# A recurrence followed by a mixture of experts: the triangular solve taken two columns at a time, on VectorE for four of the units, with its loads issued three units ahead

## The chip, the cores and the metric

The kernel runs on one core of a Trainium2 chip. The metric is the device time of one execution in microseconds (us); lower is better. Three executions of the kernel before gave 1191.62, 1196.45 and 1198.73 us, so the median is 1196.45 us.

## What is computed

The first half is a recurrence over 768 tokens for 4 batches of 8 heads of width 40. Each token reads a 40x40 state and then updates it:

```python
for t in range(S):
    y[:, :, t] = np.einsum('bhd,bhde->bhe', rt, state)
    Sa = np.einsum('bhde,bhe->bhd', state, at)
    state_decay = state * wt[:, :, None, :] - np.einsum('bhd,bhe->bhde', Sa, bt)
    state = state_decay + np.einsum('bhd,bhe->bhde', vt, kt)
```

The second half takes the 3072 rows of y (320 wide) through four experts of hidden width 1024 and adds them up with normalized weights:

```python
for e in range(E):
    h = np.maximum(x @ w1[e], 0.0)
    out += p[:, e:e + 1] * (h @ w2[e])
```

All of it is in 32-bit floating point.

## The kernel before, in words

**Units.** The 768 tokens are cut into 12 chunks of 64. A unit is one chunk of two batches (2 x 64 tokens on the 128 partitions, 8 heads), so there are 24 units; even units hold batches 0 and 1, odd units batches 2 and 3. Inside a chunk the recurrence is turned into matrix products and one unit lower triangular system per head and batch. That system is split into 32x32 blocks: `substitute` (L433) inverts the diagonal blocks, and `merge` (L456) joins them with small matmuls.

**Stages of a unit.** `within` (L335) is a generator that prepares a unit without the state: running products of the decay (`pw`, the scan L342), scaled copies of the inputs (`gp`, `a_tok`, the reciprocal L360, `n_tok` L385, `k_tok` L388), TensorE transposes of them (`turned`: `AT`, `NT`, `KT`, `RT`, `VT`), and the score blocks (`pfe`, copied by ScalarE to `F` at L412 and masked to `ET`). `substitute` copies the diagonal blocks of `F` to `blocks` (L437), spreads them with one VectorE transpose to `M` (L441), and then runs 31 steps, one column each: a product `tmp` (L450) and an addition into `Z` (L454). Step j works on (j//4 + 1) x (31 - j) elements in each partition. Unit 0 does this on VectorE, all others on GpSimd. `merge` transposes `Z` to `Qc` and `QTc` (L461, L463) on VectorE; then come the matmuls `pY` and `pQ`. `step` (L496) applies the state: `prn`, `psat`, `pxr`, the masked copies `SX`, then `pdy`, from which the outputs `Y` and the new state are made. `Y` goes to `xT`, the input of the experts, by twelve small DMAs (L600), for unit 0 by TensorE (`pxT`, L588) instead.

**The mixture.** Units 0 and 1 go through the experts one by one (`mixture_of_unit`), the others in pairs (`mixture_of_chunk`). Its pieces stand in a list `todo`; `mix(n)` emits the next n of them between the stages of the recurrence. They fill TensorE while the recurrence waits. In each iteration of the main loop (L843) there are four places for them, `gap(0)` to `gap(3)`; in iterations 1 to 3 and at the first place of iteration 4 a gap takes one piece, later two (`sparse`, L840). Four of the gaps also hold `add_weights`, five VectorE additions of 128x640 each.

**Order.** The order of every engine follows the order in which the program emits, as a list scheduler sees it: among instructions that are ready in its own model of time, the one emitted first goes first. An instruction that isn't ready there lets a later one pass. `tc.keep_in_program_order` puts one instruction behind the one emitted before it on the same engine, and nothing more. At run time each engine keeps its order. In iteration u of the main loop the unit u takes its state step, unit u+1 is merged (`run(m, 1)` ahead of `gap(1)`), unit u+2 goes through `within` and, ahead of `gap(3)`, through `substitute`. `Qc` is pinned behind `k_tok` of unit u+2, which is the VectorE instruction emitted ahead of it.

**Loads.** Every load and store is issued from SyncE's queue (SP). A unit's inputs take 20 DMAs (L188), 2 each for W, A, B and K and 6 each for V and R. W, V and R have two buffers each, A, B and K one. The first layer's weights are loaded again for every unit or chunk, in pieces of three DMAs (L237); each piece waits for the matmuls that used its buffer.

Of the kernel before, what the change touches and what calls it, by code (L numbers as in the profile page):

```python
# [7 lines left out]
FP32 = mybir.dt.float32  # L8
# [7 lines left out]
def kernel(  # L16
# [172 lines left out]

    for u in range(3):  # L190
        begin(u)
    for u, names in ((0, "WABKV"), (1, "W"), (0, "R")):
        load(units[u], names)


# [91 lines left out]

    QUADS = ((0, 0), (1, 1), (0, 1), (1, 0))

    def turn(name, src):  # L290

        p = big(name)
        for j in range(NJ):
            nc.tensor.transpose(out=p[:, j * P:(j + 1) * P], in_=src(j), identity=ident[:])
        return p

    def tok(x):
# [37 lines left out]
    def within(q):  # L335

        n = q.n
        pw = by(turn("pw", tok(n["W"]))[:], L)
        q.G = G = sb.tile([P, 2 * NJ, L], FP32, name="G", tag="G", bufs=3)
        nc.vector.memset(G[:, :, 0:1], 0.0)  # L340
        nc.scalar.copy(out=G[:, :, 1:L], in_=pw[:, :, 0:L - 1])
        ins = nc.vector.tensor_tensor_scan(  # L342
            out=G[:].rearrange("p c i -> p (c i)"), data0=G[:].rearrange("p c i -> p (c i)"),
            data1=first[:].rearrange("p c i -> p (c i)"), initial=0.0, op0=ALU.mult, op1=ALU.add,
        )
        if q.u == 1:
            tc.keep_in_program_order(ins)
        q.gl = sb.tile([P, 2 * NJ, 1], FP32, name="gl", tag="gl", bufs=4)
        nc.scalar.copy(out=q.gl[:], in_=pw[:, :, L - 1:L])
        nc.vector.tensor_tensor(out=q.gl[:], in0=q.gl[:], in1=G[:, :, L - 1:L], op=ALU.mult)  # L350
        yield

        pg = by(turn("pg", tok(G))[:], 64)[:, :, 0:D]
        gp = sb.tile([P, H, D], FP32, name="gp")
        ins = nc.vector.tensor_tensor(out=gp[:], in0=pg, in1=n["W"][:, :, 0:D], op=ALU.mult)
        if q.u == 1:
            tc.keep_in_program_order(ins)
        A = a_tok()
        nc.vector.tensor_tensor(out=A[:, :, 0:D], in0=pg, in1=n["A"][:], op=ALU.mult)
        nc.vector.reciprocal(out=gp[:], in_=gp[:])  # L360

        def turned(name, x, keep=False):
            t = sb.tile([P, NJ, P], FP32, name=name, tag=name if keep else "turned", bufs=2 if keep else 3)
            nc.scalar.copy(out=t[:].rearrange("p j t -> p (j t)"), in_=turn("p" + name, tok(x))[:])
            return t

        def turn_rv():
            q.RT = turned("RT", n["R"], True)
            return turned("VT", n["V"])

        def causal_scores(VT):
            pc = quadrants(banks("pc"), 0, BY_TOKENS, L, lambda j, s, i: (
                d_half(j, s), i, j, of_pairs(VT, d_half(j, s), j, i), of_pairs(q.RT, d_half(j, s), j, i),
            ))
            for s in range(2):
                ins = causal(of_slot(q.VC[:], s)[:, :, D:D + L], pc[s])
                if q.start:
                    tc.keep_in_program_order(ins)

        if not q.start:  # L380
            VT = turn_rv()
            yield

        q.K, q.N = k_tok(), n_tok()
        nc.vector.scalar_tensor_tensor(  # L385
            out=q.N[:, :, 0:D], in0=n["B"][:], scalar=-1.0, in1=gp[:], op0=ALU.mult, op1=ALU.mult,
        )
        nc.vector.tensor_tensor(out=q.K[:, :, 0:D], in0=n["K"][:], in1=gp[:], op=ALU.mult)  # L388
        q.VC = VCs()
        if not q.start:  # L390
            nc.scalar.copy(out=q.VC[:, :, 0:D], in_=n["V"][:, :, 0:D])
        yield

        q.AT = turned("AT", A, True)
        NT = turned("NT", q.N)
        KT = turned("KT", q.K)
        yield

        if not q.start:
            causal_scores(VT)  # L400
            yield

        p = banks("pfe")
        pf = quadrants(p, 0, BY_TOKENS, L, lambda j, s, i: (
            s, i ^ s, j, of_pairs(q.AT, s, j, i), of_pairs(NT, s, j, i),
        ))
        pe = quadrants(p, NJ * L, BY_TOKENS, L, lambda j, s, i: (
            s, i, j, of_pairs(KT, s, j, i), of_pairs(q.AT, s, j, i),
        ))
        q.F = sb.tile([P, H, L], FP32, name="F", tag="F", bufs=2)  # L410
        for s in range(2):
            nc.scalar.copy(out=of_slot(q.F[:], s), in_=pf[s])  # L412
        ET = ETs()
        for s in range(2):
            causal(of_slot(ET[:], s), pe[s])
        yield

        if q.start:
            tc.keep_in_program_order(nc.scalar.copy(out=q.VC[:, :, 0:D], in_=n["V"][:, :, 0:D]))
        q.EV = EVs()  # L420
        pev = quadrants(banks("pev"), 0, BY_TOKENS, D, lambda j, s, i: (
            i, i ^ s, j, ET[half(i), head(j, s), :], q.VC[half(i), d_head(j, s), 0:D],
        ))
        for i in range(2):
            for p in range(2):
                nc.scalar.copy(out=of_slot(q.EV[half(p)], i ^ p)[:, :, 0:D], in_=pev[i][half(p)])
        yield

        if q.start:
            causal_scores(turn_rv())  # L430
        yield

    def substitute(q, eng):  # L433

        blocks = sb.tile([P, H, Q], FP32, name="blocks")
        for i in range(P // Q):
            ins = eng.tensor_copy(out=blocks[quarter(i)], in_=q.F[quarter(i), :, quarter(i % 2)])  # L437
            tc.keep_in_program_order(ins)
        M = sb.tile([P, Q, Q], FP32, name="M")
        cols = blocks[:].rearrange("p h c -> p c h")[:, :, None, :].to_broadcast([P, Q, 4, H])  # L440
        ins = nc.vector.transpose(out=M[:], in_=cols)  # L441
        if q.u == 1:
            tc.keep_in_program_order(ins)
        q.Z = Z = sb.tile([P, Q // 4, Q], FP32, name="Z", tag="Z", bufs=2)
        tmp = sb.tile([P, Q * Q // 8], FP32, name="tmp", tag="tmp", bufs=2)
        tc.keep_in_program_order(eng.tensor_copy(out=Z[:], in_=unit_cols[:]))
        for j in range(Q - 1):
            n, m = j // 4 + 1, Q - 1 - j
            t = tmp[:, 0:n * m].rearrange("p (k r) -> p k r", k=n)
            eng.tensor_tensor(  # L450
                out=t, in0=M[:, j:j + 1, j + 1:Q].to_broadcast([P, n, m]),
                in1=Z[:, 0:n, j:j + 1].to_broadcast([P, n, m]), op=ALU.mult,
            )
            eng.tensor_tensor(out=Z[:, 0:n, j + 1:Q], in0=Z[:, 0:n, j + 1:Q], in1=t, op=ALU.add)  # L454

    def merge(q):  # L456


        Qc = sb.tile([P, H, Q], FP32, name="Qc", tag="q", bufs=2)
        QTc = sb.tile([P, H, Q], FP32, name="QTc", tag="q", bufs=2)  # L460
        tc.keep_in_program_order(nc.vector.transpose(out=dealt(Qc[:]), in_=q.Z[:]))  # L461
        tc.keep_in_program_order(
            nc.vector.transpose(  # L463
                out=QTc[:].rearrange("p h r -> p (h r)"), in_=Qc[:].rearrange("p h c -> p (h c)"),
# [31 lines left out]
    def step(q, xT):  # L496
# [82 lines left out]
        if not q.end:  # L579
            gl = q.gl[:].rearrange("p (j i) o -> p j i o", i=2)  # L580
            for i in range(2):
                x = st[i][:, :, 0:D]
                nc.vector.tensor_tensor(out=x, in0=pdy[i][:, :, 0:D], in1=x, op=ALU.add)
                nc.vector.tensor_tensor(out=x, in0=x, in1=gl[:, :, i, :].to_broadcast([P, NJ, D]), op=ALU.mult)
        if q.u == 0:
            px = big("pxT")
            for n, (g, j) in enumerate(PLACES):
                nc.tensor.matmul(  # L588
                    out=px[:, g * P:(g + 1) * P], lhsT=pick[:, n, :], rhs=Y[:, j].rearrange("p i t -> p (i t)"),
                    start=(n == 0 or PLACES[n - 1][0] != g), stop=(n + 1 == len(PLACES) or PLACES[n + 1][0] != g),  # L590
                )
            nc.scalar.copy(out=xT, in_=px[:, 0:3 * P].rearrange("p (g t) -> p g t", g=3))
# [202 lines left out]
    load(units[1], "ABKVR")  # L795
    run(ws[1], 1)
    run(ws[0], 2)
    substitute(units[0], nc.vector)
    run(ws[0], 1)
    set_pick()  # L800
    m, s = merge(units[0]), begin_step(0)
# [10 lines left out]
    for e in range(2, E):  # L812
        load_w2(e)
    run(m)
    run(s, 2)
    run(ws[1], 1)
    run(s, 1)
    run(ws[1], 1)
    run(s)
    substitute(units[1], nc.gpsimd)  # L820
    mixture_of_unit(units[0])
    normalize()
    run(ws[2], 1)
# [3 lines left out]
    mix(1)  # L827
    run(ws[2], 2)
    mix(1)
    run(ws[2], 1)  # L830
    m, s = merge(units[1]), begin_step(1)
    run(m, 1)
    substitute(units[2], nc.gpsimd)
    run(m)
    mix(1)
    run(s, 2)
    mix(1)
    w_next = ws[2]

    sparse = [4 * u + n for u in range(1, 4) for n in range(4)] + [16]  # L840

# [1 line left out]
    for u in range(1, NU):  # L843
# [2 lines left out]
        if u + 1 < NU:  # L846
            m, s_next = merge(units[u + 1]), begin_step(u + 1)
        if u + 2 < NU:
            load(begin(u + 2), srcs)
            w = within(units[u + 2])  # L850

        def gap(n):
# [5 lines left out]
        run(w, 1)  # L858
        run(w_next)
        run(s, 1)  # L860
        gap(0)

        run(w, 1)
# [6 lines left out]
        run(m, 1)  # L870
        gap(1)

        run(w, 2)
        run(m, 1)
        run(s_next, 1)
# [3 lines left out]
        run(w, 1)  # L879
        run(s_next, 1)  # L880
        if u + 2 < NU:
            substitute(units[u + 2], nc.gpsimd)
        gap(3)
        s, w_next = s_next, w
    mix(len(todo))
# [30 lines left out]
```

## Time and profile before

| | |
|---|---|
| three runs | 1191.62, 1196.45, 1198.73 us |
| the profiled execution | 1196.92 us |
| its span on the core | 1195.1 us, mean granted TensorE clock 0.97 |
| TensorE matmul (PE) busy | 1126.1 us, 94% |
| VectorE (DVE) busy | 636.1 us, 53%, 1342 instructions |
| GpSimd (POOL) busy | 575.8 us, 48%, 1681 instructions |
| ScalarE (ACT) busy | 364.6 us, 31% |
| the products of the solve on POOL, L450 | 713 instructions, 233.3 us |
| the additions of the solve on POOL, L454 | 713 instructions, 247.0 us |

The profile is of one execution. PE and PEld are TensorE's matmuls and its loading of weights, DVE is VectorE, POOL is GpSimd, ACT is ScalarE, SPq is the issuing of DMAs from SyncE. In the rows of the timeline the first two numbers are the start and the length in us; a bracket at the end tells how long the engine was idle ahead of the instruction, and what ended that. A matmul's end is modelled, so a busy PE isn't a PE at its peak. In the page's slices, each character is one fortieth of the span, about 30 us.

### The profile page before, as it was taken

What the parts mean: (1) busy time and instruction counts of PE and PEld (TensorE: products, weight loads), DVE (VectorE), ACT (ScalarE), POOL (GpSimd) and SP (SyncE); (2) the same over time, 40 slices, a digit from 0 to 9 for tenths busy, and PEclk for the clock granted to TensorE, in tenths of its full rate; (3) what the DMA queues carried; (4) which work ended last, traced back from release to release, by engine and by line L of the source; (5) the groups of instructions that cost most, each with busy time, mean ns of one, the idle gap of its engine ahead of it and who ended that gap; (6) DMA issues with size and microseconds to landing.
All of it is one profiled execution on the core that took longest, in us unless ns stands there. A gap on an engine that the chain in (4) does not pass through costs nothing.

```text
span 1195.1 us, 38873 instructions
## 1 busy us (share of the span) xinstructions
PE 1126.1 (94%) x16272; PEld 1005.5 (84%) x16272; DVE 636.1 (53%) x1342; ACT 364.6 (31%) x910; POOL 575.8 (48%) x1681
## 2 busy tenths in 40 slices
PE   3499796889999999999999999999999999989998
PEld 3487685778988989989989899899888998988897
DVE  5633364645646556566466465465556456433433
ACT  2133342323333333333333333423323333321110
POOL 3167655726536537537447447447447356350000
PEclk8689897979999999999999999999999999999999
DMA  4764433332342332333333333333333331221320
GB/s 67 200 213 93 129 67 82 79 87 65 96 91 78 102 87 72 109 74 88 110 74 88 93 91 87 90 94 88 91 91 89 92 85 63 75 72 63 102 88 12
DMA packets 220249, 108.05 MB, mean 90 GB/s; under 512 B 164090, under 2 KB 193450, under 8 KB 220074
## 3 DMA queue, kind: packets, MB, share of 16 engines
q1 hardware_dynamic: 220074, 105.56, 34.0%
q8 instruction: 129, 2.11, 0.7%
q14 instruction: 46, 0.38, 0.1%
HBM read 97.04 MB, written 3.93 MB: 84 GB/s over the span
## 4 chain that ended last, share of the span: by engine, by line
PE 84%; POOL 6%; DVE 3%; SPq 3%; issue 2%; DMA 1%; ACT 0%; DVEq 0%; POOLq 0%
PE p L727 27%; PE ph L623 27%; PE ph L615 8%; PE pdy L324 3%; POOL Z L454 3%; POOL tmp L450 3%; PE pfe L324 2%; PE prn L324 2%; SPq L188 2%; PE po L662 2%; PE psat L324 2%; PE pxr L324 2%; PE pQ L488 1%; PE pY L476 1%; PE pc L324 1%
## 5 line engine op out<-in xcount | busy, mean ns | idle before, releaser
L623 PE MATMUL ph<-xT,w1p 128*128 128x256 f32 (+1 forms) x1520 | 345.1, 380 | 0.7 <-issue 0.7
L623 PEld LDWEIGHTS ph<-xT,w1p 128*128 128x128 f32 x1520 | 275.8, 192 | 63.7 <-issue 24.9
L450 POOL TENSOR_TENSOR tmp<-M,Z 128x60 f32<-128x60 f32 (+24 forms) x713 | 233.3, 327 | 93.6 <-DVE M L441 39.6
L454 POOL TENSOR_TENSOR Z<-Z,tmp 128x60 f32<-128x60 f32 (+24 forms) x713 | 247.0, 346 | 55.9
L721 DVE TENSOR_TENSOR a<-hs 128x512 f32<-128x512 f32 x220 | 150.2, 700 | 196.1 <-ACT hs L628 196.1
L628 ACT ACTIVATE hs<-ph 128x512 f32<-128x512 f32 (+1 forms) x208 | 117.3, 564 | 318.0 <-PE ph L623 317.1
L641 DVE SCALAR_TENSOR_TENSOR osb<-p,gate,osb 128x320 f32<-128x320 f32 (+1 forms) x242 | 108.0, 484 | 129.9 <-PE p L727 122.7
L437 POOL COPY blocks<-F 32x256 f32<-32x256 f32 x92 | 36.4, 396 | 271.7 <-ACT F L412 268.8
L727 PE MATMUL p<-sums,a 128*128 128x160 f32 x1056 | 164.8, 299 | 0.0
L727 PEld LDWEIGHTS p<-sums,a 128*128 128x128 f32 x1056 | 152.9, 190 | 2.2
L615 PE MATMUL ph<-xT,w1p 64*128 64x256 f32 (+1 forms) x760 | 107.9, 399 | 0.2 <-issue 0.2
L727 PE MATMUL p<-w,hs 128*128 128x160 f32 x704 | 102.8, 299 | 0.0
L727 PE MATMUL p<-w,a 128*128 128x160 f32 x704 | 102.8, 299 | 0.0
L727 PEld LDWEIGHTS p<-w,hs 128*128 128x128 f32 x704 | 100.3, 190 | 2.2
L727 PEld LDWEIGHTS p<-w,a 128*128 128x128 f32 x704 | 98.0, 190 | 0.0
L615 PEld LDWEIGHTS ph<-xT,w1p 64*128 64x128 f32 x760 | 66.8, 189 | 12.3 <-issue 2.4
L469 POOL COPY QT<-QTc 32x256 f32<-32x256 f32 x96 | 37.9, 395 | 67.1 <-DVE QTc L463 61.1
L441 DVE STREAM_TRANSPOSE M<-blocks 128x1024 f32<-128x1024 f32 x24 | 47.2, 1966 | 30.4 <-POOL blocks L437 30.3
L461 DVE STREAM_TRANSPOSE Qc<-Z 128x256 f32<-128x256 f32 x24 | 15.1, 627 | 81.8 <-POOL Z L454 81.7
L360 DVE RECIPROCAL gp<-gp 128x320 f32<-128x320 f32 x24 | 51.4, 2143 | 0.0
L476 PE MATMUL pY<-QTc,F 32*32 32x32 f32 x768 | 17.8, 198 | 34.5 <-DVE QTc L463 34.5
L412 ACT COPY F<-pfe 128x256 f32<-128x256 f32 x48 | 15.5, 376 | 106.4 <-PE pfe L324 106.4
(136 smaller groups left out, 1375.9 us busy)
## 6 DMA issues: line engine op xcount, KB each, us to landing
w1p<-in_moe_w_dram SPq DMA_DIRECT2D x95, 512.0 KB
w1p<-in_moe_w_dram SPq DMA_DIRECT2D x190, 64.0 KB
w<-in_moe_w_dram SPq DMA_DIRECT2D x4, 1280.0 KB
sums<-in_moe_w_dram SPq DMA_DIRECT2D x9, 512.0 KB
natW<-in_w_dram SPq DMA_DIRECT2D x48, 80.0 KB
natA<-in_a_dram SPq DMA_DIRECT2D x48, 80.0 KB
natB<-in_b_dram SPq DMA_DIRECT2D x48, 80.0 KB
natK<-in_k_dram SPq DMA_DIRECT2D x48, 80.0 KB
```

What stands on the lines that cost most here:

```text
L324: nc.tensor.matmul(out=p[row][half(col), lo + at * out_cols:lo + (at + 1) * out_cols], lhsT=lhsT, rhs=rhs, start=(n == 0), stop=(n == len( ...
L360: nc.vector.reciprocal(out=gp[:], in_=gp[:])
L441: ins = nc.vector.transpose(out=M[:], in_=cols)
L450: eng.tensor_tensor(out=t, in0=M[:, j:j + 1, j + 1:Q].to_broadcast([P, n, m]), in1=Z[:, 0:n, j:j + 1].to_broadcast([P, n, m]), op=ALU.mult,)
L454: eng.tensor_tensor(out=Z[:, 0:n, j + 1:Q], in0=Z[:, 0:n, j + 1:Q], in1=t, op=ALU.add)
L469: ins = nc.gpsimd.tensor_copy(out=q.QT[quarter(i), :, quarter(i % 2)], in_=QTc[quarter(i)])
L615: nc.tensor.matmul(out=ph[i][:, f, :], lhsT=w1.last[i * DT:(i + 1) * DT, f, :], rhs=xT[i * DT:(i + 1) * DT, 2, :], start=(f == 0), stop=False,
L623: nc.tensor.matmul(out=ph[i][:, f, :], lhsT=w1.main[:, g, at * P:(at + 1) * P], rhs=xT[:, g, :], start=False, stop=(g == 1 and f == HF // ...
L628: nc.scalar.activation(out=h[:, i * HF // 2:(i + 1) * HF // 2, 0:n], in_=ph[i][:], func=ACTF.Relu,)
L641: nc.vector.scalar_tensor_tensor(out=to, in0=p, scalar=sc, in1=to, op0=ALU.mult, op1=ALU.add)
L721: nc.vector.tensor_tensor(out=t[:], in0=x, in1=y, op=op)
L727: nc.tensor.matmul(out=p[:, n * HD:(n + 1) * HD], lhsT=a[:, f, :], rhs=b[:, f, :], start=(f == 0), stop=(f == HF - 1),)
```

## The change

The solve takes two columns in each step, so there are 16 steps. A first part, always on VectorE, makes that possible: with the element just below the diagonal of each pair of columns, the second column is multiplied and added to the first (two instructions of 512 elements and a small `memset`), so that both columns of a pair can be multiplied by values known ahead of the step. A step is then one multiplication of both columns (twice the elements of one column) and a sum of the pair's two products and the old `Z`: on VectorE one `tensor_reduce` over three terms, which lie 256 elements apart, and which writes to the other of two copies of `Z`; on GpSimd two additions. On VectorE a last copy puts the rows of every other pair together. `Z` now has four planes and one buffer. The emission is cut in two at step 8.

Units 0, 3, 4 and 5 take VectorE, the others GpSimd. The second half of a unit's solve is emitted in the next iteration, behind the masked copies `SX` of the state step, and its first multiplication is pinned there. In the main loop a unit's 20 loads are emitted behind `gap(1)`, three units ahead, where they stood at the beginning of the iteration, two units ahead. Ahead of the loop the loads of unit 1's W go in front of unit 0's A, B, K, V; unit 0's state step is emitted up to its `pdy` ahead of unit 1's transposes and scores (a new `yield` ahead of `pxT`); the first merges move ahead of the last stages of the unit that follows; and some instructions of unit 1 are pinned.

```diff
-    for u, names in ((0, "WABKV"), (1, "W"), (0, "R")):
+    for u, names in ((0, "W"), (1, "W"), (0, "ABKVR")):
...
-        nc.vector.memset(G[:, :, 0:1], 0.0)
+        ins = nc.vector.memset(G[:, :, 0:1], 0.0)
+        if q.u == 1:
+            tc.keep_in_program_order(ins)
...
+        pairs = M[:].rearrange("p (c two) r -> p c two r", two=2)
+        on_diag = M[:].rearrange("p c r -> p (c r)")[:, Q + 1::2 * (Q + 1)]
+        nc.vector.memset(on_diag, 0.0)
+        Z = sb.tile([P, 4, Q // 4, Q], FP32, name="Z")
+        q.Z = Z[:, 0]
+        by_second = Z[:, 1:3].rearrange("p x k r -> p (x k) r")
+        below = M[:].rearrange("p c r -> p (c r)")[:, 1::2 * (Q + 1)]
+        nc.vector.tensor_tensor(
+            out=by_second, in0=pairs[:, :, 1, :], in1=below[:, :, None].to_broadcast([P, Q // 2, Q]), op=ALU.mult,
+        )
+        nc.vector.tensor_tensor(out=pairs[:, :, 0, :], in0=pairs[:, :, 0, :], in1=by_second, op=ALU.add)
+        at_once = eng is nc.vector
+        for x in (0, 3) if at_once else (0,):
+            tc.keep_in_program_order(eng.tensor_copy(out=Z[:, x], in_=unit_cols[:]))
+        for j in range(0, Q, 2):
+            if j == Q // 2:
+                yield
             n, m = j // 4 + 1, Q - 1 - j
...
+            here = 3 * (j // 2 % 2) if at_once else 0
+            ins = eng.tensor_tensor(
+                out=Z[:, 1:3, 0:n, j + 1:Q], in0=M[:, j:j + 2, None, j + 1:Q].to_broadcast([P, 2, n, m]),
+                in1=Z[:, here, 0:n, j:j + 2].rearrange("p k x -> p x k")[:, :, :, None].to_broadcast([P, 2, n, m]),
+                op=ALU.mult,
             )
+            if j in (0, Q // 2):
+                tc.keep_in_program_order(ins)
+            z = Z[:, :, 0:n, j + 1:Q]
+            if at_once:
+                terms = z[:, 0:3] if here == 0 else z[:, 1:4]
+                eng.tensor_reduce(out=z[:, 3 - here], in_=terms.rearrange("p x k r -> p k r x"), op=ALU.add, axis=AX.X)
+            else:
+                for x in range(1, 3):
+                    eng.tensor_tensor(out=z[:, 0], in0=z[:, 0], in1=z[:, x], op=ALU.add)
+        if at_once:
+            odd, even = (Z[:, x].rearrange("p k (r four) -> p k r four", four=4)[:, :, :, 1:3] for x in (3, 0))
+            eng.tensor_copy(out=even, in_=odd)
+        yield
...
-    run(s, 2)
-    run(ws[1], 1)
-    run(s, 1)
+    run(s, 4)
     run(ws[1], 1)
     run(s)
-    substitute(units[1], nc.gpsimd)
+    run(ws[1], 1)
+    run(substitute(units[1], nc.gpsimd))
...
-    run(ws[2], 1)
     m, s = merge(units[1]), begin_step(1)
     run(m, 1)
-    substitute(units[2], nc.gpsimd)
+    run(ws[2], 1)
+    load(begin(3), srcs)
+    run(substitute(units[2], nc.gpsimd))
...
         if u + 2 < NU:
-            load(begin(u + 2), srcs)
             w = within(units[u + 2])
...
         run(s, 1)
+        run(solve)
         gap(0)
...
+        if u + 3 < NU:
+            load(begin(u + 3), srcs)
         run(w, 2)
...
         if u + 2 < NU:
-            substitute(units[u + 2], nc.gpsimd)
+            solve = substitute(units[u + 2], nc.vector if u < 4 else nc.gpsimd)
+            run(solve, 1)
         gap(3)
```

More of the change, by code (lines that the diff above doesn't have):

```diff
@@ L288, with turn @@
     QUADS = ((0, 0), (1, 1), (0, 1), (1, 0))
-    def turn(name, src):
+    def turn(name, src, pinned=False):
         p = big(name)
         for j in range(NJ):
-            nc.tensor.transpose(out=p[:, j * P:(j + 1) * P], in_=src(j), identity=ident[:])
+            ins = nc.tensor.transpose(out=p[:, j * P:(j + 1) * P], in_=src(j), identity=ident[:])
+            if pinned and j == 0:
+                tc.keep_in_program_order(ins)
         return p
@@ L363, in turned @@
             t = sb.tile([P, NJ, P], FP32, name=name, tag=name if keep else "turned", bufs=2 if keep else 3)
-            nc.scalar.copy(out=t[:].rearrange("p j t -> p (j t)"), in_=turn("p" + name, tok(x))[:])
+            nc.scalar.copy(out=t[:].rearrange("p j t -> p (j t)"), in_=turn("p" + name, tok(x), q.u == 1)[:])
             return t
@@ L441, in substitute @@
         ins = nc.vector.transpose(out=M[:], in_=cols)
-        if q.u == 1:
+        if q.u == 1 or eng is nc.vector:
             tc.keep_in_program_order(ins)
[L444 to L447, printed above, removed]
-            n, m = j // 4 + 1, Q - 1 - j
[L449 to L452, printed above, removed]
-            )
-            eng.tensor_tensor(out=Z[:, 0:n, j + 1:Q], in0=Z[:, 0:n, j + 1:Q], in1=t, op=ALU.add)
+        pairs = M[:].rearrange("p (c two) r -> p c two r", two=2)
@@ new lines, in substitute @@
+        at_once = eng is nc.vector
[4 more added lines that the diff above has]
+                yield
+            n, m = j // 4 + 1, Q - 1 - j
+            here = 3 * (j // 2 % 2) if at_once else 0
[3 more added lines that the diff above has]
+                op=ALU.mult,
+            )
+            if j in (0, Q // 2):
+                tc.keep_in_program_order(ins)
+            z = Z[:, :, 0:n, j + 1:Q]
[5 more added lines that the diff above has]
+                    eng.tensor_tensor(out=z[:, 0], in0=z[:, 0], in1=z[:, x], op=ALU.add)
@@ L460, in merge @@
         QTc = sb.tile([P, H, Q], FP32, name="QTc", tag="q", bufs=2)
-        tc.keep_in_program_order(nc.vector.transpose(out=dealt(Qc[:]), in_=q.Z[:]))
+        tc.keep_in_program_order(nc.vector.transpose(out=dealt(Qc[:]), in_=q.Z))
         tc.keep_in_program_order(
@@ L584, in step @@
                 nc.vector.tensor_tensor(out=x, in0=x, in1=gl[:, :, i, :].to_broadcast([P, NJ, D]), op=ALU.mult)
+        yield
         if q.u == 0:
@@ L797 @@
     run(ws[0], 2)
-    substitute(units[0], nc.vector)
+    run(substitute(units[0], nc.vector))
     run(ws[0], 1)
@@ L837 @@
     mix(1)
-    w_next = ws[2]
+    w_next, solve = ws[2], iter(())
     sparse = [4 * u + n for u in range(1, 4) for n in range(4)] + [16]
```

## The prediction

> **What bounds the kernel now.** First the page: the slices of the span, and the shares of the chain that ended last.
>
> ```profile
> PE   3499796889999999999999999999999999989998
> ...
> PEclk8689897979999999999999999999999999999999
> ...
> PE 84%; POOL 6%; DVE 3%; SPq 3%; issue 2%; DMA 1%; ACT 0%; DVEq 0%; POOLq 0%
> ```
>
> TensorE is full from the ninth slice (240 us) on; a solve with fewer instructions gains nothing there while it stays hidden. Holes are in the first eight slices and near the end, and the clock row dips where they are. The timeline of TensorE, in windows around those holes, says who ended them:
>
> ```profile
> 13.98 1.09 PE L294 MATMUL pw<-ident,natW 128*128 128x128 f32 x4 [5.17 <-DMA natW<-in_w_dram]
> ...
> 144.99 0.66 PE L294 MATMUL pRT<-ident,natR 128*128 128x128 f32 x2 [5.34 <-DMA natR<-in_r_dram]
> ...
> 197.47 1.06 PE L476 MATMUL pY<-QTc,F 32*32 32x32 f32 x32 [9.10 <-DVE QTc L463]
> ...
> 242.05 1.06 PE L476 MATMUL pY<-QTc,F 32*32 32x32 f32 x32 [8.21 <-DVE QTc L463]
> ...
> 1065.31 0.69 PE L476 MATMUL pY<-QTc,F 32*32 32x32 f32 x32 [2.50 <-DVE QTc L463]
> ```
>
> Two loads come late, and three times the merge waits for a solve: units 4, 5 and 23 (a fourth is unit 0's, idle 14.7 us to 40.6). After the 9.1 us hole the same 32 matmuls take 1.06 us, not 0.69: they run at half clock. What VectorE does between the scores `F` of units 3, 4, 5 and their `Qc`, in busy time by stretch (PE, PEld, DVE, ACT, POOL):
>
> ```profile
> 126.60:154.30 27.70, 21.64 (x291) 18.11 (x282) 11.44 (x22) 8.66 (x25) 20.99 (x67) 0.88 0.56 142
> 166.22:196.20 29.98, 22.15 (x344) 19.22 (x336) 15.45 (x27) 10.90 (x30) 23.28 (x67) 0.91 0.32 56
> 209.23:240.80 31.57, 24.61 (x328) 21.30 (x320) 18.32 (x31) 11.03 (x28) 24.86 (x67) 0.96 0.33 85
> ```
>
> VectorE is half busy here already, and must now take GpSimd's part too. For costs, groups by form, then single rows of unit 0's solve and the only reduction:
>
> ```profile
> L441 DVE STREAM_TRANSPOSE M<-blocks 128x1024 f32<-128x1024 f32 x24 | 47.2, 1966 | 30.4 <-POOL blocks L437 30.3
> ...
> L463 DVE STREAM_TRANSPOSE QTc<-Qc 128x256 f32<-128x256 f32 x24 | 10.7, 445 | 0.5
> ```
>
> ```profile
> 24.11 0.19 DVE L450 TENSOR_TENSOR tmp<-M,Z 128x31 f32<-128x31 f32 x1
> 24.33 0.19 DVE L454 TENSOR_TENSOR Z<-Z,tmp 128x31 f32<-128x31 f32 x1
> ...
> 61.21 0.25 DVE L266 TENSOR_REDUCE total<-gate 128x24 f32<-128x96 f32 x1
> ```
>
> **The new solve, by itself.** In unit 0's solve, 62 instructions run from 24.11 to 39.31. Each waits for the one before; starts lie 0.21 (8 elements) to 0.27 us (76) apart: 0.20 us fixed, then about 1 ns per element. Independent ones on the same engine (`a_tok` behind `gp`, 320 elements) lie 0.40 apart, so 0.07 fixed: the dependence leaves a bubble of 0.13 us.
>
> On VectorE the 16 steps hold 816 positions. Multiplications: 16 x 0.20 + 1632 x 1.04 ns = 4.9 us. Reductions read 2448 elements, 1 KB apart. No row has a strided reduction. Lower end: L266, as quick per element as a product of its size, so 1.04 ns, 5.8 us in all. L441 reads scattered elements: (1966 - 170)/1024 = 1.75 ns against (445 - 170)/256 = 1.07 for the contiguous L463; this gives 16 x 0.20 + 4.3 = 7.5 us, and I take it, being nearest in stride. Upper end 2.5 ns, 9.3 us. [...]
>
> Preparation: two operations of 512 (0.7 each, as L721), memset 0.1, two copies 0.5; tail copy 0.2. With blocks (1.2) and `M` (2.0), from `F` to the finished `Z` it is 17.7 us of VectorE, chained. Without blocks and `M`: 14.5, where unit 0 takes 15.5 now (copy 0.26 among it). So this gains 1.0 (0 to 2.7): half the instructions, but 4080 elements instead of 3120.
>
> On GpSimd: 62 instructions of an undisturbed solve (unit 2) take 22.2 us: 0.28 fixed each, 1.5 ns per element. Now 48 instructions and 3264 elements: 13.6 + 4.9 = 18.5, plus 1.5 of preparation on VectorE ahead of it: 2.2 us sooner. For units 1, 2, 6 to 22 this is worth nothing, as other work covers it: TensorE waits under 1 us for any of them. The 1.5 us on VectorE lie beside 43 us of TensorE work per unit, of which VectorE uses 24.
>
> **Start.** Unit 0's transposes stand behind unit 1's `pw`, which waits for a load until 13.98. With that W second in SP's queue it lands about 8 us sooner; A, B, K, V move back by two DMAs (1.35 us), but are still there when used (B would land near 8.7, used at 11.83). Then `pNT` starts behind `n_tok` at 12.35 instead of 15.71: 3.4 us. The pins hold unit 1's memset and scan behind `k_tok`. With the solve: 4.4.
>
> The reordered state step: from `psat`'s end to the first expert matmul is 15.5 us now, 4.6 of it idle (3.1 an "issue" wait while the DMA engines are full). Earlier `pxr` and `pdy` add waits of 0.6 and 0.95 for ScalarE's `SaT` and VectorE's `SX`, and unit 1's transposes fill the wait for `Y`. If the issue wait comes again 0.8 is gained, if it goes 3.9; if it grows by a microsecond, nothing. I take 0.8. Unit 1's scores come 1 us later, but its solve ended 6 us early. Start: 5.2 (2.5 to 9).
>
> **Loads.** The 20 DMAs at 0.65 us are 13 us of SP's queue. Now they pass the weight pieces of two gaps, which wait on matmuls (280 us of SP's waits), and those pieces go back by at most 13 us; their slack is such a wait. Buffers: A, B and K of the unit before are used ahead of `gap(1)`. So the two waits for R go: 1.5 us at 111, and 5.3 + 0.5 at 140 to 147 with 1.3 of half clock behind it. The second is next met by unit 3's solve.
>
> **Units 3, 4, 5.** Everything of VectorE between `F` and `Qc` is in its queue ahead of `Qc`, so its sum sets the merge. Take `M` (2.0) from the stretches and add 17.7. Other ready instructions can slip into the bubbles, as now at 182 to 186, where state updates, `Y` and `n_tok` alternate; each fills 0.13 us.
> - Unit 3: 9.5 + 17.7 - 21 x 0.13 = 24.5, so `pY` at 25.7 behind `F`; now 30.9 (held up by R). TensorE's own work allows 23.7. Gain 5.2.
> - Unit 4: 13.5 + 17.7 - 26 x 0.13 = 27.8 against 30.0: gain 2.2.
> - Unit 5: 16.4 + 17.7 - 30 x 0.13 = 30.2 against 31.6: gain 1.4.
>
> GpSimd's wait is replaced by VectorE's queue, and the holes of 9.1 and 8.2 us only shrink; their half clock stays. No bubble filled costs 2.7, 3.4 and 3.9; a reduction at 1.04 ns gives 1.7 each. The second half is pinned behind `SX`, so behind TensorE's `pxr`; in its wait stand `add_weights`, then `gp`, the reciprocal and `n_tok`, which unit u+2's transposes await. `SX` is done 8 us behind `F` now, before the first half ends (11), so this costs nothing unless `pxr` is late. `Z` with one buffer: the previous `Qc` has read it long before.
>
> **End.** Unit 23 on GpSimd, 2.2 sooner and less disturbed by additions on VectorE: of 2.5 + 0.7 I take 2.5 (1 to 3.2).
>
> Sum: 5.2 + 1.5 + 5.2 + 2.2 + 1.4 + 2.5 = 18.0. The profiled execution took 1196.92 us (span 1195.1), half a microsecond over the median: 1179.
>
> **Rivals.**
> - Forecast as above, 1172 to 1186: 0.56.
> - VectorE is quicker: reduction at 1.04 ns, no issue wait in the first step. 9.1 + 1.5 + 6.5 + 3.9 + 3.1 + 3 = 27, 1170; below, to 1164, if a hole gets too short for the half clock (3.4 and 5.0 us of it). For: L266. Against: the stride. 0.23.
> - VectorE becomes the bound for units 3 to 5: no bubble is filled, so 2.5 - 1.2 - 2.5, start 2.6, loads 1.5, end 2.5: 5.4, 1191.5. The same comes of a late R all the same, if SP's queue blocks (the change then doesn't do what it says). For: VectorE would be busy without a break. 0.15.
> - Slower: the strided reduction. Each ns more per element costs 2.45 us in each of four units, 9.8 us in all; 18 us are gone at 1.75 + 1.84 = 3.6 ns. At 5 ns it would be 1211. For: no row of it. Against: twice the nearest row. 0.06.
>
> **The numbers.** A measurement of this kernel can tell about 0.5% (6 us) from no change. Faster by more: 0.56 + 0.23 + 0.06 of the third = 0.85; within: 0.09; slower: 0.06. Range 1167 to 1192: it leaves out the slower case and the farthest of the second and third.
>
> **What would show it.** Right: `pNT` near 12.4; unit 0's solve near 14.5 us; reductions of 24 to 228 elements from about 0.2 to 0.55 us; no wait for R; holes ahead of `pY` of units 4 and 5 of 5 to 8 us with VectorE busy through them; none for unit 23. Wrong: an issue wait or weight pieces arriving late near 60 us, TensorE held at `pNT` of units 5 and 6 because `n_tok` stands behind the solve, or new gaps in slices 9 to 34.

## The result, and the profile after

The changed kernel takes 1180.93 us (median of four executions, 1178.3 to 1181.41), beside 1195.51 for the kernel before in the same comparison: ratio 0.9875, 95% interval 0.9841 to 0.9909. The forecast was 1179.0, in a range of 1167 to 1192. The total came within 2 us of the forecast, in part by luck: a large term of it was wrong, and terms that it didn't have made up for that.

The page of the changed kernel: TensorE's slices, its granted clock, and the chain that ended last.

```profile
PE   4789996999999999999999999999999999999998
...
PEclk8689997999999999999999999999999999999999
...
PE 86%; DVE 5%; POOL 3%; SPq 2%; issue 2%; DMA 1%; ACT 1%; POOLq 0%; DVEq 0%; ACTq 0%
```

The chain gained two points of TensorE; GpSimd's share fell from 6% to 3%, and VectorE's rose from 3% to 5%. TensorE is full behind the seventh slice (206 us), where before it was full only behind the ninth (the forecast read it as full from the ninth on). TensorE's timeline, at the places that answer to those shown of before and at the new ones:

```profile
12.62 1.09 PE L294 MATMUL pNT<-ident,n_tok 128*128 128x128 f32 x4 [1.52 <-DVE n_tok L389]
...
78.17 1.06 PE L510 MATMUL pY<-QTc,F 32*32 32x32 f32 x32 [3.93 <-DVE QTc L497]
...
138.10 0.41 PE L294 MATMUL pRT<-ident,natR 128*128 128x128 f32 x2 [0.77 <-DMA natR<-in_r_dram]
...
184.56 1.11 PE L294 MATMUL pNT<-ident,n_tok 128*128 128x128 f32 x4 [4.72 <-DVE n_tok L389]
...
187.52 1.06 PE L510 MATMUL pY<-QTc,F 32*32 32x32 f32 x32
...
234.17 0.69 PE L510 MATMUL pY<-QTc,F 32*32 32x32 f32 x32
...
1050.32 0.69 PE L510 MATMUL pY<-QTc,F 32*32 32x32 f32 x32 [0.43 <-DVE QTc L497]
```

The holes of 9.1 and 8.2 us ahead of `pY` of units 4 and 5 are gone (the rows at 187 and 234 have no bracket), and that of unit 23 is down from 2.50 to 0.43 us. The wait for R of 5.3 us is down to 0.8. But two holes are new: unit 1's merge waits 3.9 us for its solve, which GpSimd does, and the transposes of unit 5's `n_tok` wait 4.7 us for VectorE. A third new one, of 4.5 us, ends at 203.4, at the experts of unit 3's rows. The chain of waits there leaves its last 3 us as "issue":

```profile
197.12 3.28 DMA xT<-Y
200.40 2.96 issue
203.37 3.02 PE ph L651 x8
```

The semaphores of the trace fill that in. TensorE's sequencer waits from 198.43 to 203.31 for two counts; the last one came at 203.28, from a DMA of the weights `w1p`. These weights stood in SyncE's queue behind the twelve small DMAs of `xT`, and those behind inputs of a later unit; the queue issues almost without a break from 148 to 209 us:

```profile
183.92 3.90 SPq L188 DMA_DIRECT2D natV<-in_v_dram  x6
187.86 1.26 SPq L188 DMA_DIRECT2D natR<-in_r_dram  x2
189.22 10.21 SPq L636 DMA_DIRECT2D xT<-Y  x12
199.53 3.44 SPq L237 DMA_DIRECT2D w1p<-in_moe_w_dram  x6
```

In the kernel before, the same weights were issued from 196.8 on, and TensorE needed them only at 209.3.

VectorE between `F` and `Qc` of units 3, 4 and 5 (busy PE, PEld, DVE, ACT, POOL, then the clock, by stretch):

```profile
123.90:147.60 23.70, 21.59 (x313) 18.25 (x305) 22.65 (x64) 9.97 (x29) 0.00 (x0) 1.00 0.64 122
157.70:185.00 27.30, 21.87 (x310) 18.53 (x303) 26.25 (x69) 9.93 (x29) 0.00 (x0) 0.98 0.40 78
198.60:231.70 33.10, 26.97 (x286) 22.27 (x279) 28.07 (x74) 9.59 (x26) 0.00 (x0) 0.85 0.43 113
```

For units 3 and 4 it is 96% busy, where before it was 41% and 52%: here VectorE is the bound, as the forecast's sum assumed. For unit 5 it is 85% busy and idle for 5.0 us, 4.2 of them in one wait for the experts behind the hole at 203. Single rows of unit 0's solve:

```profile
27.05 0.41 DVE L480 TENSOR_REDUCE Z<-Z 128x76 f32<-128x228 f32 x1
...
33.24 0.19 DVE L480 TENSOR_REDUCE Z<-Z 128x8 f32<-128x24 f32 x1
```

From 24 to 228 elements the reduction goes from 0.19 to 0.41 us, 1.1 ns per element. That is about what the products of the same solve cost (L470: 0.19 us for 16 elements, 0.32 for 152, 1.0 ns per element); the 1 KB between its terms shows no cost of its own.

Where the 15.4 us between the two profiled executions came from, by the times of the first expert matmul, of `F`, and of the last matmul:

| stretch | forecast | measured |
|---|---|---|
| to the first expert matmul (61.85 to 51.66) | 5.2 | 10.2 |
| to unit 3's `F`, all in all (125.9 to 123.3) | 6.7 | 2.6 |
| unit 3's `F` to unit 4's (39.6 to 33.8) | 5.2 | 5.9 |
| unit 4's to unit 5's | 2.2 | 2.1 |
| unit 5's to unit 6's | 1.4 | 1.8 |
| unit 6's to the end | 2.5 | 3.0 |
| sum, without the first row | 18.0 | 15.4 |

The second row takes in the first, and the forecast's 1.5 us for the R wait at 111.

### The profile page after: what moved, and what is told of

Same layout as the page of the kernel before. It is cut to its first block, busy times and chain, and to the rows that moved or that the text cites. A ratio compares the mean times of both kernels' runs of the same rounds, so it can differ in the third digit from the quotient of the medians.

```text
span 1179.7 us, 38554 instructions
## 1 busy us (share of the span) xinstructions
PE 1129.8 (96%) x16272; PEld 1005.5 (85%) x16272; DVE 698.1 (59%) x1503; ACT 364.5 (31%) x910; POOL 462.4 (39%) x1200
## 4 chain that ended last, share of the span: by engine, by line
PE 86%; DVE 5%; POOL 3%; SPq 2%; issue 2%; DMA 1%; ACT 1%; POOLq 0%; DVEq 0%; ACTq 0%
PE p L763 27%; PE ph L659 27%; PE ph L651 8%; PE pdy L326 3%; PE po L698 2%; PE pfe L326 2%; PE prn L326 2%; POOL Z L483 2%; PE psat L326 2%; PE pxr L326 2%; SPq L188 1%; PE pQ L522 1%; PE pY L510 1%; POOL Z L470 1%; PE pc L326 1%
## 5 line engine op out<-in xcount | busy, mean ns | idle before, releaser
L483 POOL TENSOR_TENSOR Z<-Z 128x54 f32<-128x54 f32 (+14 forms) x640 | 217.4, 340 | 50.2
L470 POOL TENSOR_TENSOR Z<-M,Z 128x62 f32<-128x62 f32 (+7 forms) x320 | 154.2, 482 | 89.5 <-DVE M L461 66.0
L441 POOL COPY blocks<-F 32x256 f32<-32x256 f32 x80 | 32.3, 404 | 276.6 <-ACT F L416 274.1
L592 ACT COPY RS<-pxr 64x256 f32<-64x256 f32 x88 | 32.2, 366 | 44.3 <-issue 25.3
L698 PE MATMUL po<-w,hs 128*128 128x320 f32 x128 | 44.0, 500 | 0.0
```

Source lines behind the costliest of these rows:

```text
L470: ins = eng.tensor_tensor(out=Z[:, 1:3, 0:n, j + 1:Q], in0=M[:, j:j + 2, None, j + 1:Q].to_broadcast([P, 2, n, m]), in1=Z[:, here, 0:n, j: ...
L483: eng.tensor_tensor(out=z[:, 0], in0=z[:, 0], in1=z[:, x], op=ALU.add)
L698: nc.tensor.matmul(out=po[:], lhsT=hs[e][f // HF][:, f % HF, 0:P], rhs=w2_sb[e][:, f, :], start=(f == 0), stop=(f == NF - 1),)
```

## The experiments

Times are medians of three rounds (four or more executions); ratios are against the kernel before, with a 95% interval.

| kernel | us | ratio |
|---|---|---|
| changed | 1180.93 | 0.9875 [0.9841, 0.9909] |
| unit 1 on VectorE | 1175.35 | 0.9827 [0.9798, 0.9855] |
| units 3 to 5 on GpSimd | 1185.29 | 0.9918 [0.9887, 0.995] |
| one column at a time | 1187.85 | 0.9931 [0.9907, 0.9955] |
| loads two ahead | 1181.26 | 0.9881 [0.9853, 0.9909] |
| first loads in the old order | 1183.6 | 0.9897 [0.9871, 0.9923] |
| first step in the old order | 1173.93 | 0.9824 [0.9793, 0.9854] |
| additions in place of the reduction | 1182.7 | 0.9897 [0.9868, 0.9927] |
| unit 1 on VectorE, weights moved | 1170.92 | 0.9794 [0.9765, 0.9822] |
| the two above and the old first step | 1172.61 | 0.9824 [0.9803, 0.9845] |
| before, with the new first step alone | 1196.9 | 1.0019 [1.0006, 1.0033] |

The theory was that the start gained twice the forecast and lost nearly all of the surplus at unit 1's merge, and that units 3 to 5 gained by VectorE's sum, as forecast. The rivals: the hole at unit 1 costs nothing of its own; GpSimd would have done as well for units 3 to 5; the parts of the start don't add up.

**Unit 1's solve on VectorE.**

```diff
-    run(substitute(units[1], nc.gpsimd))
+    run(substitute(units[1], nc.vector))
```

> Unit 1's solve goes to VectorE as well, nothing else changes. Theory A (the start gained 10.3 us up to the first expert matmul, and 9 of them went into the wait for unit 1's solve on GpSimd: 3.9 us idle at 74.6 to 78.2 and about 5 us of half clock behind it): F of unit 1 is there at 51.3, VectorE needs some 16 us for the solve and has about 8 us of other work in between, so QTc comes at 68 to 75 instead of 78.1, the hole and the half clock go, and the kernel takes 1172 to 1176 us. Theory B (another wait stands right behind it: gp, a_tok and n_tok of unit 2 wait in VectorE's queue behind the solve, and TensorE holds at pNT of unit 2): a hole of 3 us or more at 65 to 70, and 1179 to 1184 us.

The hole is gone, and the half clock behind it (`pY` takes 0.69 us; in the changed kernel 1.06, at a granted clock of 0.50):

```profile
74.99 0.69 PE L510 MATMUL pY<-QTc,F 32*32 32x32 f32 x32
...
179.22 1.11 PE L294 MATMUL pNT<-ident,n_tok 128*128 128x128 f32 x4 [4.81 <-DVE n_tok L389]
```

Unit 3's `F` comes at 114.0 instead of 123.3, so hole and half clock had cost most of 9.3 us there (the first expert matmul is 1.1 us earlier in this execution). A longer wait for R (3.1 us at 130.6) takes 4 of it by unit 4's `F`, but the hole ahead of unit 3's experts is then gone, and unit 6's `F` is 8.7 us earlier. The medians differ by 5.6. The hole of 4.8 at unit 5's tokens is untouched.

**The first step in the old order**, all else as changed.

```diff
-    run(s, 4)
+    run(s, 2)
     run(ws[1], 1)
-    run(s)
+    run(s, 1)
     run(ws[1], 1)
+    run(s)
```

> The changed kernel with the order of the first step put back (two parts of unit 0's side work, then one part of weights, and so on, as before), all else as changed. Theory A (what the reorder saved ahead of the first expert matmul was eaten at unit 1's pY, which waits for GpSimd's solve either way): first expert matmul 4 us later, near 55.7 us, unit 1's hole shorter by about as much, total 1176 to 1181. Theory B (the reorder is worth its 4.3 us to the end): 1184 to 1187.

The total is lower even than the first theory had it, and one number of that theory is wrong in a telling way: the first expert matmul did not come 4 us later.

```profile
46.99 0.82 PE L624 MATMUL pxT<-Y,sums 128*128 128x128 f32 x5 [0.79 <-DVE Y L607]
48.97 1.01 PE L624 MATMUL pxT<-Y,sums 128*128 128x128 f32 x7 [1.16 <-issue]
...
51.55 1.23 PE L651 MATMUL ph<-xT,w1p 64*128 64x128 f32 x8
...
75.38 0.69 PE L510 MATMUL pY<-QTc,F 32*32 32x32 f32 x32
```

It starts at 51.55, as in the changed kernel (51.66). So the reorder bought nothing there, and made unit 1's `F` 6.1 us later (50.6 against 44.5), because the matmuls of `pdy` and `pxT` now stand ahead of `pfe`. Unit 6's `F` keeps 8.4 of the 9.1 us by which unit 3's `F` is earlier here. With the old order unit 1's solve on GpSimd, unchanged, is in time: no bracket at 75.38. This one part of the change makes the whole slower, by 7 us of the medians: the two intervals against the kernel before overlap slightly, but each of the four executions here (1172.2 to 1177.7) is below each of the changed kernel's.

**Before, with the new first step alone.** The same edit the other way round.

> The kernel before with the new order of the first step alone; nothing is left out. Theory A (as the prediction had it: the first expert matmul comes 0.8 to 3.9 us earlier, unit 1's scores come 1 us later and its solve has 6 us to spare): 1191.5 to 1195. Theory B (as the changed kernel with the old order says: unit 1's scores come about 6 us later for nothing or little gained ahead of the first expert matmul, and its merge then holds TensorE): unit 1's F near 57, a wait at its pY, total 1196 to 1203.

Neither theory holds whole. The first expert matmul comes 3.3 us earlier (58.54), unit 1's `F` 4.8 later (57.1), and its merge waits only 0.9 us. Unit 6's `F` keeps 3.0 us of this and unit 23's 3.9; but the profiled span is 1195.0, as before, and the median of 20 executions is 2 us longer than that of the kernel before. In this execution the hole of unit 23's `pY` (2.46 us, before 2.50) was followed by half clock. TensorE's rows by stretch, with this kernel first and the kernel before second (busy PE, granted clock, DMA share, GB/s):

```profile
1058.10:1061.30 3.20, 0.86 (x7) 1.00 0.07 17
1061.30:1071.50 10.20, 10.08 (x146) 0.50 0.24 72
```

```profile
1062.00:1065.30 3.30, 0.81 (x6) 1.00 0.07 17
1065.30:1075.50 10.20, 9.48 (x171) 1.00 0.36 94
```

Why the other executions lost it as well isn't shown.

**First loads in the old order.**

```diff
-    for u, names in ((0, "W"), (1, "W"), (0, "ABKVR")):
+    for u, names in ((0, "WABKV"), (1, "W"), (0, "R")):
```

> The changed kernel with the order of the first loads put back (all of units 0's W, A, B, K and V, then unit 1's W, then unit 0's R), all else as changed. Theory A (the 3.06 us that the first TensorE instruction came earlier are worth all of themselves, since everything behind it, unit 1's F and the hole at its pY too, moves as one): first expert matmul near 54.8 us, the hole at unit 1's pY still near 4 us, total 1183 to 1185. Theory B (the later waits, unit 1's hole or the loads, take it up): 1180 to 1182.

`pNT` starts at 15.85 instead of 12.62, the first expert matmul at 54.07 (2.4 later), unit 1's hole is 4.55 us. The total agrees with theory A, but 2.7 us lie inside the intervals; the trace carries it.

**Units 3 to 5 on GpSimd.**

```diff
-            solve = substitute(units[u + 2], nc.vector if u < 4 else nc.gpsimd)
+            solve = substitute(units[u + 2], nc.gpsimd)
```

> Units 3, 4 and 5 are solved on GpSimd, two columns at a time, all else as in the changed kernel. Theory A (VectorE's queue is as long as GpSimd's solve would be): from F to Qc 26, 28 and 30 us for the three units (before: 28.4, 30.6, 32.2; changed: 24.3, 27.9, 33.7), and the time stays within 3 us of the changed kernel's, 1178 to 1184 us. Theory B (moving these units to VectorE is what made the middle faster): the holes ahead of pY of units 4 and 5 come back to 7 us or more with their half clock, 1187 to 1192 us.

Between the two. The holes of before are back, but smaller:

```profile
188.08 1.06 PE L510 MATMUL pY<-QTc,F 32*32 32x32 f32 x32 [7.03 <-DVE QTc L497]
...
232.51 1.06 PE L510 MATMUL pY<-QTc,F 32*32 32x32 f32 x32 [6.17 <-DVE QTc L497]
```

From unit 3's `F` to unit 6's it takes 128.3 us; before 133.3, changed 123.5. So of the 9.8 us gained in this stretch the move to VectorE is worth about half. The other half is there without it; two columns, loads and the split on GpSimd aren't told apart in it. The total says 4.4 us for the move.

**One column at a time**, on the same engines and in the same places.

```diff
-        for j in range(0, Q, 2):
+        for j in range(Q - 1):
...
-                eng.tensor_reduce(out=z[:, 3 - here], in_=terms.rearrange("p x k r -> p k r x"), op=ALU.add, axis=AX.X)
...
+            eng.tensor_tensor(out=Z[:, 0:n, j + 1:Q], in0=Z[:, 0:n, j + 1:Q], in1=t, op=ALU.add)
```

> The old solve, one column at a time, in the new schedule: same engines, same halves, same pins, no preparation on VectorE. Theory A (the form of the solve is worth what its rows say): unit 0's solve takes 15.5 us instead of 12.5, unit 1's hole grows from 3.9 to about 6, units 3 and 4 cost 2 to 3 us each, the last unit's hole comes back (2.5): 1189 to 1197 us. Theory B (the order and the loads made the gain, and the solve is covered except in unit 0): 1182 to 1186 us.

Between the two theories, and 7 us slower than the changed kernel: unit 0's `F` to `Qc` is 19.7 us instead of 16.9, unit 3's `F` to unit 6's 126.7, and of the two merges that wait for GpSimd, unit 1's is later still (5.7 us instead of 3.9) and unit 23's is late again:

```profile
82.37 0.85 PE L487 MATMUL pY<-QTc,F 32*32 32x32 f32 x24 [5.74 <-DVE QTc L474]
...
1056.45 1.06 PE L487 MATMUL pY<-QTc,F 32*32 32x32 f32 x32 [2.49 <-DVE QTc L474]
```

**Additions in place of the reduction**, on VectorE too.

```diff
-        at_once = eng is nc.vector
+        at_once = False
```

> The changed kernel with two additions in place of the one reduction per pair on VectorE too (units 0, 3, 4 and 5), all else as changed. Theory A (the additions cost 8.1 us per solve by the rows of before, the reductions 5.7 as the trace of after has them, and all four solves stand on the path): 2.3 us per unit, unit 0's Qc near 36.5 us, total 1184 to 1189. Theory B (the additions are as quick, or what they cost is covered by other waits): 1180 to 1183.

From start to start unit 0's 32 additions take 7.9 us, the 16 reductions of the changed kernel 5.9. `F` to `Qc` grows by 1.9 us in unit 0 and by 1.3, 1.3 and 1.6 in units 3 to 5, and the profiled span by 6.4. The profiled execution is the slowest of the four, and the median grows by 1.8 only: the total doesn't decide, the trace speaks for A with less than its 2.3 per unit.

**Loads two ahead**, at the head of the iteration.

```diff
-    load(begin(3), srcs)
...
+            load(begin(u + 2), srcs)
...
-        if u + 3 < NU:
-            load(begin(u + 3), srcs)
```

> Loads two units ahead at the head of the iteration, as before, all else as in the changed kernel. Theory A (the early loads end the waits for R but hold back the xT DMAs of unit 3 in SyncE's queue): the waits for R come back, about 1.5 and 5 to 7 us; the wait of 4.5 us for xT at 199 goes with its half clock: 1180 to 1185 us. Theory B (the loads are the main gain in the middle): 1187 to 1191 us. Theory C (the early loads do more harm than good): 1173 to 1177 us.

No difference in the total. The wait for R is back, and the hole at 203 is gone:

```profile
143.06 0.66 PE L294 MATMUL pRT<-ident,natR 128*128 128x128 f32 x2 [3.28 <-DMA natR<-in_r_dram]
...
204.87 1.13 PE L651 MATMUL ph<-xT,w1p 64*128 64x256 f32 x8
```

This looks as if the earlier loads delayed the weights, but SyncE's queue is the same at this place:

```profile
184.55 3.90 SPq L188 DMA_DIRECT2D natV<-in_v_dram  x6
188.49 1.25 SPq L188 DMA_DIRECT2D natR<-in_r_dram  x2
189.86 8.89 SPq L636 DMA_DIRECT2D xT<-Y  x12
198.85 3.43 SPq L237 DMA_DIRECT2D w1p<-in_moe_w_dram  x6
```

The DMA that ended the wait in the changed kernel lands at 203.2 here and 203.3 there. TensorE only comes to these experts later, at 204.9 instead of 198.9, since it has waited elsewhere, for R among others. So one wait stands in place of another; that the earlier loads delay the weights isn't shown.

**Unit 1 on VectorE, and the weights moved.** In the changed kernel, VectorE's rows between unit 4's solve and unit 5's `n_tok` are these:

```profile
176.27 0.19 DVE L480 TENSOR_REDUCE Z<-Z 128x8 f32<-128x24 f32 x1
176.38 2.29 DVE L735 TENSOR_TENSOR sums<-w 128x640 f32<-128x640 f32 x3
178.58 1.55 DVE L735 TENSOR_TENSOR w<-w 128x640 f32<-128x640 f32 x2
180.05 2.15 DVE L364 RECIPROCAL gp<-gp 128x320 f32<-128x320 f32 x1
```

The solve holds up `add_weights` (3.8 us), which stands ahead of the reciprocal that `n_tok` needs. Emitted one gap later, it is out of the way:

```diff
-    weights_at = {4 * 2 + 2: 0, 4 * 3 + 0: 1, 4 * 3 + 2: 2, 4 * 3 + 3: 3}
+    weights_at = {4 * 2 + 2: 0, 4 * 3 + 1: 1, 4 * 3 + 2: 2, 4 * 3 + 3: 3}
...
-    run(substitute(units[1], nc.gpsimd))
+    run(substitute(units[1], nc.vector))
```

> The kernel with unit 1's solve on VectorE too, and the second part of the weights' addition of the fourth unit's first step moved one place later, so that it doesn't stand between unit 4's F and its Qc on VectorE; nothing is left out. Theory A (the hole of 4.8 us at the transposes of unit 5's tokens, and the half clock behind it, come from VectorE doing this addition before it gets to the tokens): that hole goes or falls below 2 us, total 1169 to 1173. Theory B (VectorE's sum stays, so the hole only moves): 1174 to 1178.

```profile
175.66 0.66 PE L294 MATMUL pNT<-ident,n_tok 128*128 128x128 f32 x4 [1.68 <-DVE n_tok L389]
...
182.21 1.06 PE L522 MATMUL pQ<-Yq,Qc 32*32 32x32 f32 x32 [2.92 <-DVE VC L333]
```

The hole at the tokens falls from 4.8 to 1.7 us, a new one of 2.9 comes behind VectorE at `pQ`, and that ahead of unit 4's `pdy` is 4.4 us at 209.4 (1.4 in the changed kernel). This is the best median of all, 1170.92; its interval overlaps that of unit 1 on VectorE alone.

**All three together.**

> The changed kernel with three edits of the runs before this one together: unit 1's solve on VectorE, the second part of the weights' addition one place later, and the order of the first step put back; nothing is left out. Theory A (the order of the first step costs only through unit 1, whose F it makes 6 us later; with unit 1 on VectorE that F is covered, or nearly): unit 1's Qc 3 to 6 us earlier than 71.5, but TensorE is not held by it either way: 1168 to 1172, no different from the kernel with the two other edits. Theory B (the 6 us are on the path whatever engine solves, since units 2 and 3 follow unit 1): 1163 to 1167.

Theory A: the old first step adds nothing once VectorE solves unit 1 (1172.61). Unit 1's `Qc` is 1.6 us earlier (3 to 6 were expected), unit 3's `F` 4.1 later. Both edits cure the same hole. The hole ahead of unit 3's experts is there too, and in this trace the view names the weights:

```profile
195.17 2.32 PE L651 MATMUL ph<-xT,w1p 64*128 64x256 f32 x8 [2.97 <-DMA w1p<-in_moe_w_dram]
```

## Why the prediction was right or wrong

- **VectorE's solve.** 16 multiplications 4.9 us: measured 4.7. Reductions 7.5: measured 5.9. The row taken for the stride, `M`'s transpose at 1.75 ns per scattered element, was the wrong neighbour; L266, an ordinary reduction, was the right one, and the lower end (5.8) the right number. Unit 0's solve: 14.5 forecast, 12.5 measured. Taking the reduction was right: by the rows of before the additions would take 32 x 0.20 + 1632 x 1.04 ns = 8.1 us, 0.6 more than its 7.5; measured, it beats them by 2.0 (5.9 against 7.9).
- **Start, up to the first expert matmul.** 5.2 forecast, 10.2 measured. The load order gave 3.1 (`pNT` 15.71 to 12.62) where 3.4 stood. The solve, from `blocks` to `Qc`, gave 2.8 where 1.0 stood, most of it the reductions. The rest, 4.3, lies between the end of `psat` and `ph` (15.4 to 11.1). The forecast ascribed 0.8 to 3.9 to the reorder; with the old order this stretch is 11.4, so nearly all of the 4.3 is there without it. The issue waits of 3.1 and 0.7 us became one of 1.2, and the half clock ends at 47.5, where before it ended at 50.7 and stood again from 57.5 to 67.8; what ends such a wait isn't in the profile and stays open. In the kernel before, the reorder did bring 3.3.
- **The step that failed:** "Unit 1's scores come 1 us later, but its solve ended 6 us early." They came 6.1 us later: the forecast counted the reorder's own waits and not the matmuls that moved in front of `pfe`: `pxr` and `pdy` hold TensorE from 40.8 to 45.8, at half clock, where `pxr` alone takes 0.7 in the old order, and `pxT` another 1.4. And the 6 us to spare were measured to a merge that stands 24 to 27 us behind the first expert matmul; that moved ahead by 10 us and took the cover with it. With the old order it is down to half a microsecond (`QTc` is done at 74.9, `pY` starts at 75.4). So the start's gain of 10.2, with 1.5 from the R wait at 111, lost 9.1 at unit 1, and 2.6 was left.
- **Units 3, 4, 5.** Forecast `Qc` 24.5, 27.8 and 30.2 us behind the end of `F`; measured 23.7, 27.3 and 33.0. The gains of 5.2, 2.2 and 1.4 were 5.9, 2.1 and 1.8. The method (VectorE's busy time, plus the solve, less the bubbles that others fill) holds for units 3 and 4, where VectorE is 96% busy; two errors offset there, the reductions 1.6 us too dear in each solve and 1.0 us of idle time left out. In unit 5 it fails: VectorE is idle for 5.0 us, and `Qc` comes later behind `F` than before (31.6). That the gain came out at 1.8 all the same is luck: the hole of 8.2 us at `pY` gave way to the shorter one ahead of the experts. Crediting all to VectorE was wrong: with GpSimd half of it is there.
- **The holes.** Forecast to shrink to 5 to 8 us at `pY`; they moved: 4.7 at `n_tok`, 4.5 ahead of unit 3's experts. Both stood in the forecast. It named `add_weights` and `n_tok` as queued behind the solve, and weight pieces that arrive late (near 60 us) as a sign of being wrong, and costed both at nothing. For the weights it counted on the slack of the kernel before; they were issued 2.8 us later (199.5 against 196.8), but TensorE came for them 10 us earlier.
- **Loads.** The R waits did go, as forecast (1.5 us at 111, and 5.3 to 0.8), but the runs show no net gain of them.
- **End.** 2.5 forecast, 3.0 measured; one column at a time brings the hole back.
- **Rivals.** The quicker VectorE was right in its operation and wrong in its total (1170), since unit 1 took the gain: without that hole the kernel is at 1171 to 1175. The third, VectorE as the bound with no bubble filled, would have `Qc` at 27.2 and 31.2 us in units 3 and 4 (the 2.7 and 3.4 added), or at 25.6 and 29.6 with the reductions at their measured cost; 23.7 and 27.3 were measured, so VectorE is the bound there, but not so long. SyncE's queue, which it named too, held up weights and not R. The slower one, a strided reduction at over 3.6 ns per element, is refuted at 1.1.

## What to carry to other kernels

When a stage is brought forward, whatever was hidden beside it loses cover by as much: recompute every "spare" from the new place of the work that waits, and count the busy time, not only the waits, of all that a reorder puts in front of an early producer. When an engine takes over a serial chain, list what shares its queue and who waits for that (here `add_weights` and `n_tok`), and do the same for the DMA queue. A change of several parts can win by 1.2% and still hold a part that loses 0.6%; taking the parts out one at a time finds it.

## What the hardware did that was not expected

A reduction over three terms that lie 1 KB apart runs at 1.1 ns per element read (0.19 us for 24, 0.41 us for 228), hardly slower than the products of the same solve (1.0).

Behind unit 1's hole of 3.9 us in the changed kernel TensorE ran at half clock for 10.2 us, while it was busy by its records (busy PE, clock, DMA share, GB/s, by stretch):

```profile
74.80:78.20 3.40, 0.03 (x2) 1.00 1.03 307
78.20:81.60 3.40, 3.40 (x38) 0.50 0.83 233
81.60:85.00 3.40, 3.40 (x36) 0.50 0.86 228
85.00:88.40 3.40, 3.40 (x8) 0.50 0.71 114
88.40:91.80 3.40, 3.40 (x83) 1.00 0.34 55
```

These three stretches of 3.4 us at half clock cost about 5 us (an estimate: half of 10.2), more than the hole.

In these runs the length of a hole didn't tell what followed it. In the changed kernel half clock stood from 115.7 to 119.1 us at a hole of 1.2 us (it ends at 115.6), from 184.0 to 194.2 at the one of 4.7 ahead of unit 5's `n_tok`, and from 201.1 to 207.9 at the one of 4.5 ahead of unit 3's experts. With unit 1 on VectorE a hole of 1.3 us (it ends at 66.0) drew none: the four matmuls of `pNT` behind it take 0.63 us, where 1.11 was measured at half clock. The hole of 2.5 us at unit 23 drew none in one execution (clock 1.00) and 10.2 us in another (0.50), as shown above. What decides this isn't shown, nor is a length below which a hole is too short for half clock, on which the lower end of the quicker rival counted.
